# A delta-rule attention with two MLPs: the opening in one given order on all engines, the state in SBUF, PSUM as two pairs, three merged insertions a chunk

## The chip, the cores and the metric

The kernel runs on 1 core of a Trainium2 chip. The metric is the device time of one execution in microseconds (us). The engines are TensorE (PE, matmuls), VectorE (DVE), ScalarE (ACT), GpSimd (POOL) and SyncE (SP, which here only issues DMAs). Each engine works through its own instruction queue in order and waits on semaphores of the others.

## The reference

Four batches with eight heads go through a delta rule over 768 tokens, one 48 x 48 state per batch and head. Its output, laid out as 3072 tokens by 384, goes through two MLPs with a hidden width of 2048.

```python
k_n = k / (norm(k) + 1e-06)
for t in range(S):                      # S = 768
    y[:, :, t] = q_t @ state
    v_old = state^T k_t
    state = state + beta_t * outer(k_t, v_t - v_old)
x = y as (3072, 384)
h = x @ w_in ; g = 0 if h <= -1, h if h >= 1, else (h + 1) ** 2 / 4 ; x = g @ w_out
h = x @ w_in2; g = max(h, 0) ** 2                                   ; x = g @ w_out2
```

The weights arrive as 64-bit floats, so that each must be turned into 32-bit words on the chip first.

## The kernel before

**Attention.** The tokens are cut into 12 chunks of 64, and two chunks make a group. For each chunk there are these pieces of PE work: `keys_gram` (kk, the keys' Gram matrix), `scores` (kq), `ks` (state times keys, subtracted from the values in kv), `tr` (the solved triangular matrix times kv), `qs` (the queries' part of yy), `ku` (the update of the state), `pu` (the scores' part of yy), and two `xt` (transposes of the result into the MLP's input xh, xl). For each group there is a triangular solve, `tri`: transposes of the Gram matrix on DVE (`begin`, tile gm), nine small operations with a square root on ACT (`pre`), 30 elimination steps with two operations each (`steps`; on DVE for group 0, on POOL for the others), and transposes back (`turned`, tiles tt and tq). Then `join1` (z, copied to zs by ACT) and `join2` (x) join the two 32-token halves of a chunk. The state is summed up in two PSUM banks (`s_ps`) and copied to the SBUF tile st after each chunk.

**MLP.** 24 units of 128 tokens form 9 blocks of two or three units (`UNITS`) in layer 0 and 8 blocks of three in layer 1. A step x (called a unit of work in the code after) handles one of 16 slices f of the hidden width for one block: `hidden` makes h with 9 matmuls (each operand is split into a high and a low part, and three of the four products are taken), the activation runs over ACT and DVE (r, g), then g is split into gh (ACT) and gl (DVE), and two steps later (`LAG`) `out1` or `out2` adds 9 matmuls into three accumulators acc0 to acc2. After 16 steps `evac` copies the accumulators to a tile e and sends them out.

**Weights.** Each of the 32 layer-0 tiles (128 x 384) comes as a raw 64-bit tile by DMA. ACT prepares its two words (two instructions, L185 and L189), DVE joins them to a 32-bit word (L196, tile wl), ACT casts the high part (L207), DVE subtracts it to get the low part (L211). At most two raw loads are under way (`FLIGHT`), and the beta loads are issued by ACT's queue.

**What sets the order.** Attention is inserted between the steps of the MLP at slots, two slots a step: `put_a` (exa) for PE work and `put` (exb) for the rest. PE's order is that of the code everywhere. For the other engines a scheduler, which fills their queues by its own timeline, decides from chunk 0's join on; only the loads, the Gram products and the first solve stand in a given order. The weights' stages are fed in by `more_w1`.

**PSUM.** Eight banks: two for the state, acc0 to acc2, h, and one pair (att0, att1) for all attention products.

Of the kernel before, what the change touches and what calls it, by code (L numbers as in the profile page):

```python
# [23 lines left out]
UNITS = [2, 2, 3, 3, 3, 3, 3, 2, 3]  # L24
# [3 lines left out]
def kernel(  # L28
# [9 lines left out]
    nc = tc.nc  # L38
# [16 lines left out]
    EAGER = 18  # L55
    AHEAD = 8
    FLIGHT = 2
# [5 lines left out]
    HEAD = 6  # L63
# [36 lines left out]
    def pair(shape, name):  # L100
        tags = PAIRS[0]
        if start[0]:
            tags = PAIRS[turn[0] % 2]
            turn[0] += 1
        return [ps.tile(shape, F32, tag=t, name=name) for t in tags]

    def single(shape, name):
        tag = (SINGLES if start[0] else PAIRS[0])[turn[1] % 2]
        turn[1] += 1
        return ps.tile(shape, F32, tag=tag, name=name)  # L110
# [21 lines left out]
    def load_kg(c):  # L132
        if c >= NCH:
            return
        t = kqg[c] = ring.tile([P, 2, H, T], F32, tag="kqg", bufs=2, name="kqg")
# [17 lines left out]
    def load_bet():  # L153
        src = beta.rearrange("(b o r) g (s t) -> o s b r g t", b=B2, o=2, s=2)
        for o in range(2):
            for s in range(2):
                for b2 in range(B2):
                    p = 64 * o + L * s + GC * H * b2
                    nc.scalar.dma_start(bet[p:p + GC * H], src[o, s, b2, 0:GC * H])

    raws = {}
    sent = []

    def load_w(x, key):
# [5 lines left out]
        ins = nc.sync.dma_start(  # L170
            raw.rearrange("p a b -> p (a b)"), (w1, w2)[w][f, i].bitcast(I32)
        ).ins
        if w == 0:
            sent.append(ins)
            if len(sent) > FLIGHT:
                tc.add_manual_dep(
                    ins, sent[-1 - FLIGHT].name,
                    mybir.DependencyInfo(mybir.DependencyClass.Sync, mybir.DependencyReason.DATA),
                    reason="at most FLIGHT weight loads under way",
                )  # L180

    def convert_stages(key, box):
        def s0():
            raw = box["raw"] = raws.pop(key)
            nc.scalar.activation(  # L185
                raw[:, :, 1].bitcast(F32), raw[:, :, 1].bitcast(F32), AF.Prelu,
                scale=2.0 ** -112, alpha=2.0 ** 32,
            )
# [4 lines left out]
        def s1():  # L193
            raw = box.pop("raw")
            box["t"] = tmp("wl", WL)
            nc.vector.scalar_tensor_tensor(  # L196
                box["t"].bitcast(I32), raw[:, :, 1], 3, raw[:, :, 0],
                ALU.logical_shift_left, ALU.bitwise_or,
            )

        return [s0, s1]

    def part_stages(key, box):
        _, f, i = key

        def s3():
            nc.scalar.copy(weight(i, f)[0], box["t"])  # L207

        def s4():
            hi, lo = weight(i, f)  # L210
            nc.vector.tensor_sub(lo, box["t"], hi.bitcast(F32))  # L211

        return convert_stages(key, box) + [s3, s4]
# [3 lines left out]
    def weight_items(w):  # L217

        keys = [(w, f, i) for f in range(NF) for i in range(2)]
        if w == 0:  # L220
            keys.sort(key=lambda k: (k[1] + LAG * k[2], -k[2]))

        def item(x):
            _, f, i = keys[x]
            box = {}
            if w == 0:
                r = part_stages(keys[x], box)
            else:
                r = convert_stages(keys[x], box)
                r.append(lambda: nc.sync.dma_start(w2f[f, :, i], box["t"]))  # L230
            s1 = r[1]
            r[1] = lambda: (s1(), ahead(x + 1 + (RAW if w else AHEAD)))
# [4 lines left out]
        def ahead(end):  # L237
            while todo and todo[0][0] < end:
                load_w(*todo.pop(0))
# [57 lines left out]
    def keys_gram(c, late=False):  # L297
# [4 lines left out]
        o_ = pair([P, H, 2 * L], "kk")  # L302
# [39 lines left out]
    def scores(c, late=False):  # L342

        p_ = pt[c] = ring.tile([P, B2, H, T], F32, tag="pt", bufs=1, name="pt")
        o_ = pair([P, H, T], "kq")
# [5 lines left out]
        for b2 in range(B2):  # L351
            if late:
                nc.scalar.copy(p_[:, b2], o_[b2])
            else:
                nc.vector.tensor_mul(p_[:, b2], o_[b2], by)

        def keep():
            for b2 in range(B2):
                nc.gpsimd.tensor_mul(p_[:, b2], p_[:, b2], by)

        return keep

    def tri(n, eng):
# [9 lines left out]
        def begin():  # L373
            nc.vector.transpose(gm.rearrange("p j i -> p i j"), packed)
# [51 lines left out]
    def turned(n):  # L426
        tag, bufs = ("gm", 1) if n else ("kqt", 2)
        tq[n] = ring.tile([P, B2, GC, H, L], F32, tag=tag, bufs=bufs, name="tq")
        nc.vector.transpose(tt[n][..., 0:L].rearrange(lanes), tx)
        nc.vector.transpose(tq[n].rearrange(lanes), tx.rearrange("p j i -> p i j"))  # L430
# [14 lines left out]
    def join2(n, js):  # L445
        o_ = pair([P, len(js), H, L], "x")
# [16 lines left out]
    def chunk_steps(c):  # L463
# [3 lines left out]
        def ks():  # L467
            o_ = pair([P, H, D], "ks")
# [7 lines left out]
        def tr():  # L476
            o_ = pair([P, H, D], "tr")
# [6 lines left out]
        def qs():  # L484
            o_ = t["y"] = pair([P, H, D], "yy")
# [7 lines left out]
            load_kq(c + 2)  # L493

        def ku():
            if c == NCH - 1:
                return
            flat = kvt[c].rearrange("p x h d -> p (x h d)")
            w = 64 if c == 0 else D
            each(lambda h, b2, o: mm(  # L500
                s_ps[o][rows(b2, w), h],
                flat[rows(b2 ^ o), DM * o + D * h:DM * o + D * h + w],
                kvt[c][rows(b2 ^ o), 2 + o, h],
                c == 0 and h == 0, c == NCH - 2,
            ))
            nc.vector.tensor_copy(st[:, 0], s_ps[0])
            t["st"] = nc.scalar.copy(st[:, 1], s_ps[1]).ins

        def pu():
            if c == 0:  # L510
                t["y"] = pair([P, H, D], "yy")
            if c == NCH - 1:
                for b2 in range(B2):
                    nc.scalar.copy(kvt[c][:, b2], t["y"][b2])
                t["y"] = pair([P, H, D], "yy")
            o_ = t["y"]


            each(lambda h, b2, o: mm(
                o_[b2][rows(o), h], pt[c][rows(b2 ^ o), b2, h], kvt[c][rows(b2 ^ o), 2 + o, h],  # L520
                c in (0, NCH - 1) and h == 0, behind=t.get("st") if h + b2 + o == 0 else None,
# [3 lines left out]
        def yy():  # L525
            to = kvt[c][:, 0:2]
            if c == 0:
                to = wp.tile([P, 2, H, D], F32, tag=f"w1{NF - 1}", name="y")
            for b2 in range(B2):
                if c == NCH - 1:  # L530
                    nc.vector.tensor_add(to[:, b2], to[:, b2], t["y"][b2])
                else:
                    nc.scalar.copy(to[:, b2], t["y"][b2])
            t["to"] = to

        def qk():
            qs()
            ku()

        def py():  # L540
# [23 lines left out]
        if c == 0:  # L564
            return tr, py, lambda: (ku(), done()), xt
        return ks, tr, qk, py, xt
# [17 lines left out]
    def hidden(layer, n, f):  # L584
        w = xh[n].shape[2]
        many = start[0] or (layer, n) >= (0, NB - 1) or n == 0 and f < MANY
        bank = ("h", "att0", "att1")[f % 3] if many else "h"
# [9 lines left out]
        if layer == 0:  # L597
            marks[0] = nc.scalar.activation(r, h, AF.Relu, bias=one)  # L598
            marks[1] = nc.vector.tensor_scalar(g, r, 2.0, 0.5, ALU.min, ALU.mult)  # L599
# [333 lines left out]
```

## Time and profile before

| what | us |
| --- | --- |
| three runs | 1102.3, 1111.05, 1114.37 |
| median | 1111.05 |
| profiled execution, device time | 1104.04 |
| its span from first to last instruction | 1102.3 |
| busy: PE, DVE, ACT, POOL | 965.9, 623.1, 500.0, 272.3 |
| mean granted clock of PE | 0.981 of full speed |

The share of busy time is a mean over stages with different limits. So the rows below are taken by stage: the opening up to the first MLP matmul, block zero of the MLP, the rest of layer 0, and layer 1. A busy time counts the instruction's time on the engine, with what it waits for a port in it.

### The profile page before, as it was taken

Reading aid. Unit: us, or ns where it says so; the run is one execution under the profiler, and the core shown is the slowest. Engines: PE = TensorE matmul, PEld = TensorE weight load, DVE = VectorE, ACT = ScalarE, POOL = GpSimd, SP = SyncE. Lnnn points to the kernel's source line nnn. Section 1 sums busy time; section 2 is a strip of 40 time slices with the busy share of each in tenths; the row PEclk is TensorE's granted clock in tenths of the full one; section 3 lists DMA queues with packets and bytes.
Section 4 is the critical chain, followed back from the end, with each engine's and each line's share of the span. In section 5 each row is a group of like instructions: output and inputs, shape, how many; then the busy total and the mean of one; then the engine's idle time right before and its main releaser. Section 6 shows DMA issues by size and latency. Waiting matters only on the chain.

```text
span 1102.3 us, 28998 instructions
## 1 busy us (share of the span) xinstructions
PE 965.9 (88%) x12456; PEld 934.0 (85%) x12456; DVE 623.1 (57%) x1121; ACT 500.0 (45%) x1025; POOL 272.3 (25%) x385
## 2 busy tenths in 40 slices
PE   2103698989989899999899999999999999999998
PEld 2103588978988889889899999999999999999998
DVE  1868966757756664576554577744434343434333
ACT  1555545545546345554555555433333333333332
POOL 1318602833811760058000022310101010101000
PEclk9999899999999899999999999999999999999999
DMA  8871223542335134144201122301001010000000
GB/s 167 232 214 52 59 52 97 146 119 72 75 112 155 31 96 115 33 127 124 74 3 42 63 65 84 103 1 43 21 23 44 1 44 1 23 1 22 1 22 22
DMA packets 53128, 76.67 MB, mean 70 GB/s; under 512 B 20616, under 2 KB 40456, under 8 KB 53000
## 3 DMA queue, kind: packets, MB, share of 16 engines
q1 hardware_dynamic: 52104, 74.73, 24.5%
q8 instruction: 97, 1.59, 0.6%
q10 hardware_dynamic: 896, 0.10, 0.1%
q14 instruction: 31, 0.25, 0.1%
HBM read 59.08 MB, written 15.73 MB: 68 GB/s over the span
## 4 chain that ended last, share of the span: by engine, by line
PE 69%; DVE 12%; DMA 9%; ACT 4%; issue 3%; POOL 2%; SPq 1%; DVEq 0%; ACTq 0%
PE h L574 31%; PE acc L574 31%; DMA raw<-in_w_dram 5%; PE yy L289 2%; DVE g L601 2%; DVE g L599 2%; DMA x<-e 2%; DVE wl L196 1%; DVE w L211 1%; DMA bet<-in_beta_dram 1%; DVE gl L610 1%; PE kq L289 1%; POOL t L412 1%; DMA kv<-in_kv_dram 1%; POOL tx L416 1%
## 5 line engine op out<-in xcount | busy, mean ns | idle before, releaser
L574 PE MATMUL h<-xh,w 128*128 128x384 f32 (+1 forms) x1632 | 322.6, 334 | 4.5 <-ACT r L598 3.5
L574 PEld LDWEIGHTS h<-xh,w 128*128 128x128 f32 x1632 | 278.1, 193 | 7.9 <-ACT r L598 4.3
L610 DVE TENSOR_TENSOR gl<-g,gh 128x384 fp32r<-128x384 f32 (+1 forms) x272 | 167.0, 614 | 136.3 <-ACT gh L609 130.8
L609 ACT CAST gh<-g 128x384 fp32r<-128x384 f32 (+1 forms) x272 | 134.5, 494 | 191.0 <-DVE g L601 88.8
L574 PE MATMUL h<-xl,w 128*128 128x384 f32 (+1 forms) x816 | 180.4, 330 | 0.0
L574 PE MATMUL acc<-gh,w 128*128 128x384 f32 (+1 forms) x864 | 167.7, 329 | 12.3 <-DVE e L617 8.0
L604 DVE TENSOR_TENSOR g<-r 128x384 f32<-128x384 f32 x128 | 71.3, 557 | 157.7 <-ACT r L603 157.6
L574 PE MATMUL acc<-w,gh 128*128 128x384 f32 x768 | 155.6, 337 | 1.9 <-DVE e L617 1.9
L574 PEld LDWEIGHTS acc<-gh,w 128*128 128x128 f32 x864 | 138.8, 191 | 17.5 <-DVE e L617 8.6
L603 ACT ACTIVATE r<-h,zero 128x384 f32<-128x384 f32 x128 | 74.4, 581 | 166.5 <-PE h L574 166.5
L574 PEld LDWEIGHTS h<-xl,w 128*128 128x128 f32 x816 | 142.4, 191 | 0.0
L574 PEld LDWEIGHTS acc<-w,gh 128*128 128x128 f32 x768 | 136.3, 188 | 2.2 <-ACT gh L609 2.2
L598 ACT ACTIVATE r<-h,one 128x384 f32<-128x384 f32 (+1 forms) x144 | 78.5, 545 | 83.0 <-PE h L574 81.4
L601 DVE SCALAR_TENSOR_TENSOR g<-r,g 128x384 f32<-128x384 f32 (+1 forms) x144 | 85.1, 591 | 46.0 <-ACT g L600 44.3
L599 DVE TENSOR_SCALAR g<-r 128x384 f32<-128x384 f32 (+1 forms) x144 | 66.1, 459 | 75.9 <-ACT r L598 75.2
L600 ACT ACTIVATE g<-g 128x384 f32<-128x384 f32 (+1 forms) x144 | 70.3, 488 | 66.2 <-DVE g L599 65.6
L574 PE MATMUL acc<-gl,w 128*128 128x384 f32 (+1 forms) x432 | 92.6, 323 | 6.4 <-DVE gl L610 6.4
L412 POOL TENSOR_TENSOR t<-tx,gm 128x30 f32<-128x30 f32 (+9 forms) x150 | 91.8, 612 | 17.1 <-DVE tx L402 5.8
L660 POOL CAST xh<-x2r 128x1152 fp32r<-128x1152 f32 x8 | 9.4, 1173 | 346.7 <-PE h L574 346.6
L416 POOL TENSOR_TENSOR tx<-tx,t 128x30 f32<-128x30 f32 (+9 forms) x150 | 90.5, 603 | 11.7 <-DVE tx L403 0.2
L574 PE MATMUL acc<-w,gl 128*128 128x384 f32 x384 | 88.0, 337 | 0.0
L574 PEld LDWEIGHTS acc<-gl,w 128*128 128x128 f32 x432 | 73.2, 192 | 7.2 <-DVE gl L610 7.2
(101 smaller groups left out, 880.5 us busy)
## 6 DMA issues: line engine op xcount, KB each, us to landing
raw<-in_w_dram SPq DMA_DIRECT2D x64, 384.0 KB, 3.7
kqt<-in_kq_dram SPq DMA_DIRECT2D x24, 384.0 KB, 6.5
w2f<-wl SPq DMA_DIRECT2D x32, 192.0 KB, 3.7
w2r<-w2f SPq DMA_DIRECT2D x16, 384.0 KB, 3.5
kv<-in_kv_dram SPq DMA_DIRECT2D x12, 384.0 KB, 3.4
x2r<-x SPq DMA_DIRECT2D x8, 576.0 KB, 4.3
out_dram<-e SPq DMA_DIRECT2D x24, 192.0 KB, 2.0
kqg<-in_kq_dram SPq DMA_DIRECT2D x40, 96.0 KB, 3.8
```

The costliest lines, as they stand in the source:

```text
L289: ins = nc.tensor.matmul(o, l, r, start=start, stop=stop, skip_group_check=True).ins
L412: eng.tensor_mul(t, x[:, 0:j, j:j + 1].to_broadcast([P, j, w]), gm[:, j:j + 1, j + 1:L].to_broadcast([P, j, w]),)
L416: eng.tensor_add(rest, rest, t)
L574: nc.tensor.matmul(o, *((r, l) if swap else (l, r)), **flags)
L598: marks[0] = nc.scalar.activation(r, h, AF.Relu, bias=one)
L599: marks[1] = nc.vector.tensor_scalar(g, r, 2.0, 0.5, ALU.min, ALU.mult)
L600: nc.scalar.activation(g, g, AF.Square)
L601: nc.vector.scalar_tensor_tensor(g, r, -1.0, g, ALU.add, ALU.max)
L603: marks[0] = nc.scalar.activation(r, h, AF.Relu, bias=zero)
L604: marks[1] = nc.vector.tensor_mul(g, r, r)
L609: nc.scalar.copy(ghi, g)
L610: nc.vector.tensor_sub(glo, g, ghi.bitcast(F32))
```

## The change

1. **The opening in one given order.** All engines follow the order of the code up to the end of block zero (16 steps). ACT issues no DMA any more; the beta loads go group by group through SP. The raw loads stand one after the other in SP's queue, without the limit of two. ACT prepares 18 raw tiles between the solve and zs, and the first three weight tiles are cast and subtracted by POOL. In block zero the function `between` puts two more tiles into each step: tile a is cast by ACT, tile b by POOL, and DVE joins and subtracts both.
2. **The state in SBUF.** `ku` writes its product to a PSUM pair, and DVE adds it to st (four instructions of 48 partitions; copies for chunk 0).
3. **PSUM as two pairs**, A (a0, a1) and Z (b0, b1). `ks` uses A and `scores` Z; `qs` uses Z and `tr` A; `ku` uses A and `pu` adds to Z. The other tiles rotate over all four. In layer 1 h rotates over five banks instead of three.
4. **Three merged insertions a chunk** in place of five: `one` (ks and scores), `two` (qs and tr), `three` (ku, pu and the copies).
5. The Gram tiles are evacuated by ACT and masked by POOL (`late=True`) throughout. The transposes of a solve are cut into quarters, and those back are spread over four slots, from the fifth slot ahead of the join on. The evacuation e has two buffers of its own (`ev`) for two of three accumulators. `UNITS` has its third two-unit block at place three instead of place eight.

```diff
-UNITS = [2, 2, 3, 3, 3, 3, 3, 2, 3]
+UNITS = [2, 2, 2, 3, 3, 3, 3, 3, 3]
...
-    s_ps = [ps.tile([P, H, D], F32, name=f"sps{i}") for i in range(2)]
...
-    PAIRS = [("att0", "att1"), ("acc0", "acc1")]
-    SINGLES = ["acc2", "h"]
...
+    A, Z = ("a0", "a1"), ("b0", "b1")
...
     def turned(n):
...
+        q = [slice(x * L // 4, (x + 1) * L // 4) for x in range(4)]
+        return [
+            lambda t=t, o=o, i=i: nc.vector.transpose(t[:, i], o[:, i])
+            for t, o in zip(to, of) for i in q
+        ]
...
+        def one():
+            o_ = pair([P, H, D], "ks", A)
...
+            keep = scores(c, Z)
             for b2 in range(B2):
                 r = kvt[c][:, 2 + b2]
                 nc.vector.tensor_sub(r, r, o_[b2])
+            keep()
...
+        def two():
+            o_ = t["y"] = pair([P, H, D], "yy", Z)
...
+            tr()
...
+            k_ = pair([P, H, D], "ku", tags)
             each(lambda h, b2, o: mm(
...
+                k_[o][rows(b2, D), h], flat[rows(b2 ^ o), o, D * h:D * (h + 1)],
+                kvt[c][rows(b2 ^ o), 2 + o, h], h == 0,
             ))
-            nc.vector.tensor_copy(st[:, 0], s_ps[0])
-            t["st"] = nc.scalar.copy(st[:, 1], s_ps[1]).ins
...
+                            nc.vector.tensor_add(st[r, o], st[r, o], k_[o][r])
...
+        def three():
             ku()
...
     def evac(i, o, dst):
-        e = ring.tile(list(o.shape), F32, tag="wl", bufs=WL, name="e")
+        tag, bufs = ("wl", WL) if i == 2 else ("ev", 2)
+        e = ring.tile(list(o.shape), F32, tag=tag, bufs=bufs, name="e")
...
+    def between(f):
+        a, b = (tiles + [None] * NW)[2 * f:2 * f + 2]
...
+            if x == 0:
+                if last_low:
+                    lower(last_low.pop(), V)
+                if a is not None:
+                    make(a)
+                some(2)
+            elif x == 1:
+                if a is not None:
+                    upper(a, nc.scalar.copy)
+                if b is not None:
+                    make(b)
+                    upper(b, G.tensor_copy)
+                    last_low.append(b)
+            elif x == 2:
+                some(1)
+            elif a is not None:
+                lower(a, V)
...
         go(steps)
-        turned(0)
+        for x in range(EARLY - 2):
+            whole_bits(x)
+        value(0)
         go(masks)
...
+            put(0, z - 5, *later(*[lambda fs=fs: go(fs) for fs in in_pairs(lambda: turned(g))]))
...
+        for x in range(NF):
+            unit(x, between(x))
+    with tc.manual_schedule(engines={mybir.EngineType.PE}):
+        for x in range(NF, total):
+            unit(x)
```

`make` is DVE's join, `upper` the cast, `lower` the subtraction, `halves` and `whole_bits` ACT's two preparing instructions, `some(m)` the next m of those for the last twelve tiles.

ACT's queue at its start, before and then after. In the names st is the solve's small tile behind the square root, tt and pt are copies out of PSUM, bet is beta.

```order
L159 DMA bet<-in_beta_dram 16x6x32 x8
L712 ACT_TABLE_LOAD
L712 ACTIVATE st<-one,zero 128x1
L332 COPY tt<-kk 128x8x32 x2
L185 ACTIVATE raw<-raw 128x384
L189 ACTIVATE raw<-raw 128x384
L332 COPY tt<-kk 128x8x32 x2
L185 ACTIVATE raw<-raw 128x384
L189 ACTIVATE raw<-raw 128x384
L267 ACTIVATE st_319<-gm,tiny 128x32
```

```order
L789 ACT_TABLE_LOAD
L789 ACTIVATE st<-one,zero 128x1
L329 COPY tt<-kk 128x8x32 x4
L264 ACTIVATE st_345<-gm,tiny 128x32
L326 COPY tt<-kk 128x8x32
L329 COPY tt<-kk 128x8x32
```

The beta loads and two raw tiles stood ahead of the square root; now nothing but the copies of the first two chunks does. All 18 raw tiles come behind it, and right behind them zs (L449).

DVE's queue in block zero, before from the evacuation of the first step's h, and then after. L599 and L606 are the first operation on r, L601 and L609 the second, L610 and L620 make gl; L196 and L188 are the joins, L211 and L217 the subtractions.

```order
L599 TENSOR_SCALAR g<-r 128x256
L196 SCALAR_TENSOR_TENSOR wl<-raw 128x384
L211 TENSOR_TENSOR w_1094<-wl,w_1094 128x384
L211 TENSOR_TENSOR w_1103<-wl,w_1103 128x384
L601 SCALAR_TENSOR_TENSOR g<-r,g 128x256
L196 SCALAR_TENSOR_TENSOR wl<-raw 128x384
L211 TENSOR_TENSOR w_1142<-wl,w_1142 128x384
L196 SCALAR_TENSOR_TENSOR wl<-raw 128x384
L599 TENSOR_SCALAR g<-r 128x256
L610 TENSOR_TENSOR gl<-g,gh 128x256
```

```order
L403 TENSOR_TENSOR tx<-gm,st_689 128x512
L404 COPY tx<-st_689 128x32
L606 TENSOR_SCALAR g<-r 128x256
L188 SCALAR_TENSOR_TENSOR wl<-raw 128x384
L609 SCALAR_TENSOR_TENSOR g<-r,g 128x256
L188 SCALAR_TENSOR_TENSOR wl<-raw 128x384
L620 TENSOR_TENSOR gl<-g,gh 128x256
L217 TENSOR_TENSOR w_949<-wl,w_949 128x384
L519 COPY st<-ku 48x384 x2
L606 TENSOR_SCALAR g<-r 128x256
```

The weights' work was as dense before, but about half of it stood ahead of the first step and nearly all the rest in the next seven; now two tiles go with each step up to the fifteenth, and the second solve's preparation (up to L404) stands ahead of the first step.

PE's queue around the first two insertions of chunk 2, before and then after; h, acc and w are the MLP's tiles.

```order
L289 MATMUL ks<-st,kqt 64x48 x32
L574 MATMUL h<-xh,w_905 128x256 x6
L574 MATMUL h<-xl,w_905 128x256 x3
...
L289 MATMUL kq<-kqt 64x64 x32
L574 MATMUL h<-xh,w_919 128x256 x6
```

```order
L286 MATMUL ks<-st,kqt 64x48 x32
L286 MATMUL kq<-kqt 64x64 x32
L580 MATMUL h<-xh,w_1535 128x256 x6
L580 MATMUL h<-xl,w_1535 128x256 x3
...
L286 MATMUL yy<-st,kqt 64x48 x32
L286 MATMUL tr<-kv,tt 64x48 x32
```

kq moved up to ks, into the other pair of banks; in the same way qs now stands right ahead of tr.

## Rows read from the trace of the kernel before

**Rows 1.** Busy by stretch: length, each engine's busy us (instructions), clock, DMA share, GB/s
```profile
0.00:66.00 66.00, 13.37 (x640) 11.06 (x640) 37.93 (x79) 23.69 (x54) 14.37 (x33) 1.00 0.82 201
...
88.00:140.00 52.00, 26.93 (x454) 23.57 (x458) 49.32 (x80) 27.48 (x62) 37.15 (x50) 0.93 0.15 39
106.00:172.00 66.00, 53.56 (x1110) 49.20 (x1111) 53.33 (x102) 34.91 (x83) 20.79 (x29) 0.92 0.26 58
172.00:700.00 528.00, 493.86 (x8233) 470.13 (x8231) 337.56 (x618) 274.39 (x573) 183.21 (x272) 0.97 0.31 86
700.00:1102.00 402.00, 397.49 (x2277) 397.19 (x2277) 167.66 (x282) 143.64 (x267) 30.19 (x17) 1.00 0.07 23
```
**Rows 2.** Timeline, first solve: start, us, engine, line, tiles [idle before <-releaser]
```profile
17.57 2.12 DVE L374 STREAM_TRANSPOSE gm<-tt 128x1024 f32<-128x1024 f32 x1
...
26.26 0.54 ACT L185 ACTIVATE raw<-raw 128x384 f32<-128x384 f32 x1 [9.06 <-DMA raw<-in_w_dram]
...
28.54 0.35 ACT L267 ACTIVATE st<-gm,tiny 128x32 f32<-128x32 f32 x1
...
34.23 0.18 DVE L412 TENSOR_TENSOR t<-tx,gm 128x30 f32<-128x30 f32 x1
...
63.05 1.96 DVE L430 STREAM_TRANSPOSE tq<-tx 128x1024 f32<-128x1024 f32 x1
```
**Rows 3.** Timeline of ACT around zs, and the chain's last raw tile
```profile
76.86 0.54 ACT L185 ACTIVATE raw<-raw 128x384 f32<-128x384 f32 x1 [0.69 <-DMA raw<-in_w_dram]
...
77.73 0.37 ACT L443 ACTIVATE zs<-z 128x256 f32<-128x256 f32 x1
...
84.12 3.80 DMA raw<-in_w_dram
```
**Rows 4.** Timeline of PE and ACT from zs to the first MLP matmul
```profile
84.84 2.29 PE L289 MATMUL tr<-kv,tt 64*64 64x48 f32 x64 [5.61 <-POOL tx L416]
...
93.94 1.95 PE L289 MATMUL yy<-kv,pt 64*64 64x48 f32 x62 [0.74 <-DVE kv L482]
...
102.79 0.85 ACT L533 COPY y<-yy 128x384 f32<-128x384 f32 x2
...
103.31 1.54 PE L552 MATMUL xt<-ident,y 128*128 128x128 f32 x6 [7.42 <-ACT y L533]
105.86 1.41 PE L574 MATMUL h<-xh,w 128*128 128x256 f32 x5 [1.00 <-DVE xl L555]
```
**Rows 5.** DVE's groups, 88 to 140 us: count, busy us, mean ns, idle before
```profile
L196 DVE SCALAR_TENSOR_TENSOR wl<-raw 128x384 int32<-128x384 int32 x26 | 21.2, 826 | 0.0
```
**Rows 6.** DVE's groups from 140 to 172 us, when POOL is idle
```profile
L610 DVE TENSOR_TENSOR gl<-g,gh 128x256 fp32r<-128x256 f32 x10 | 4.2, 423 | 3.2 <-ACT gh L609 2.7 <-PE kq L289 0.5
...
L599 DVE TENSOR_SCALAR g<-r 128x256 f32<-128x256 f32 x9 | 2.6, 294 | 6.1 <-ACT r L598 6.1
...
L211 DVE TENSOR_TENSOR w<-wl,w 128x384 fp32r<-128x384 f32 x2 | 1.0, 552 | 0.0
```
**Rows 7.** PE's waits, 172 to 700 us: us in total, times, longest
```profile
PE acc L574 <- DVE e L617: 8.0, 4, 2.9
PE z L289 <- DVE tt L429: 6.9, 4, 3.2
PE z L289 <- DVE tq L430: 5.9, 4, 1.5
PE kq L289 <- DVE kv L474: 5.6, 4, 2.8
```
**Rows 8.** Timeline of PE, the first matmuls of block one
```profile
171.81 0.84 PE L574 MATMUL h<-xh,w 128*128 128x256 f32 x6
```
**Rows 9.** PE's groups, 172 to 700 us, the Gram products of six chunks
```profile
L289 PE MATMUL kk<-kqg 48*32 48x64 f32 x768 | 9.4, 225 | 1.5 <-issue 1.5
```
**Rows 10.** Timeline, third solve: its transposes on DVE and POOL's last step
```profile
179.44 2.18 DVE L374 STREAM_TRANSPOSE gm<-tt 128x1024 f32<-128x1024 f32 x1 [0.29 <-ACT tt L456]
...
228.57 0.28 POOL L416 TENSOR_TENSOR tx<-tx,t 128x30 f32<-128x30 f32 x1
```

More of the change, by code (lines that the diff above doesn't have):

```diff
@@ L169, in load_w @@
         raw = raws[key] = pool.tile([P, DM, 2], I32, tag=tag, bufs=bufs, name="raw")
[L170 to L180, printed above, removed]
+        nc.sync.dma_start(raw.rearrange("p a b -> p (a b)"), (w1, w2)[w][f, i].bitcast(I32))
     def convert_stages(key, box):
@@ L191, in s0, with joined_words, halves, whole_bits @@
             )
[L193 to L213, printed above, removed]
-    w2f = dram.tile([NF, P, 2, DM], F32, name="w2f", bufs=1)
[L217 to L221, printed above, removed]
+        return high, low
+    def joined_words(t, raw):
+        nc.vector.scalar_tensor_tensor(
+            t.bitcast(I32), raw[:, :, 1], 3, raw[:, :, 0],
+            ALU.logical_shift_left, ALU.bitwise_or,
+        )
+    w2f = dram.tile([NF, P, 2, DM], F32, name="w2f", bufs=1)
+    order = [(0, f, i) for f in range(NF) for i in range(2)]
+    order.sort(key=lambda k: (k[1] + LAG * k[2], -k[2]))
+    words = {}
+    def halves(x):
+        return sign_bits(raws[order[x]])
+    def whole_bits(x):
+        for f in halves(x):
+            f()
+    def make(x):
+        words[x] = tmp("wl", WL)
+        joined_words(words[x], raws.pop(order[x]))
+    def upper(x, copy):
+        _, f, i = order[x]
+        copy(weight(i, f)[0], words[x])
+    def lower(x, eng):
+        _, f, i = order[x]
+        hi, lo = weight(i, f)
+        eng.tensor_sub(lo, words.pop(x), hi.bitcast(F32))
+    def weight_items():
+        keys = [(1, f, i) for f in range(NF) for i in range(2)]
         def item(x):
@@ L683 @@
     V, G = nc.vector, nc.gpsimd
-    first1, w1s = weight_items(0)
-    first2, w2s = weight_items(1)
-    w1f = flow(w1s)
-    w1f.reverse()
+    first2, w2s = weight_items()
+    whole = list(range(GC))
+    SL = 2 * NF
     SPREAD = 3
-    behind = [nullcontext]
-    def more_w1(m=1):
-        with behind[0]():
-            for _ in range(m):
-                if w1f:
-                    w1f.pop()()
-    whole = list(range(GC))
+    NW = len(order)
+    EARLY, READY = 20, 3
+    exa, exb = {}, {}
@@ new lines, with some, part @@
+    todo1 = [f for x in range(EARLY, NW) for f in (lambda x=x: halves(x)[0](), lambda x=x: halves(x)[1]())]
+    todo1.reverse()
+    tiles = list(range(READY, NW))
+    last_low = []
+    def some(m):
+        for _ in range(m):
+            if todo1:
+                todo1.pop()()
+    def between(f):
+        a, b = (tiles + [None] * NW)[2 * f:2 * f + 2]
+        def part(x):
+            if x == 0:
[15 more added lines that the diff above has]
+                lower(a, V)
+        return part
@@ new lines, in put, with later, one_, in_pairs @@
+    def put(n, slot, *fs):
+        for i, f in enumerate(fs):
+            exb.setdefault(SL * n + slot + i, []).append(f)
+    def later(*fs):
+        def one_(f):
+            with tc.issue_after(marks[0].ins), tc.issue_after(marks[1].ins):
+                f()
+        return [lambda f=f: one_(f) for f in fs]
+    def in_pairs(fs):
+        box = []
+        def piece(i):
+            if not box:
+                box.extend(fs())
+            go(box[2 * i:2 * i + 2])
+        return [[lambda i=i: piece(i)] for i in range(4)]
@@ new lines, in put_a, with run, out_, unit @@
+    def put_a(n, slot, f):
+        exa.setdefault(SL * n + slot, []).append(f)
+    def run(ex, x):
+        for f in ex.pop(x, ()):
+            f()
+    blocks = [(0, n) for n in range(NB)] + [(1, n) for n in range(NM)]
+    total = NF * len(blocks)
+    def out_(x):
+        g, f = divmod(x, NF)
+        (out1, out2)[blocks[g][0]](blocks[g][1], f)
+    def unit(x, between=lambda x: None):
+        g, f = divmod(x, NF)
+        rest = hidden(*blocks[g], f, between)
+        run(exa, 2 * x)
+        rest()
+        run(exb, 2 * x)
+        if x >= LAG:
+            out_(x - LAG)
+        run(exa, 2 * x + 1)
+        run(exb, 2 * x + 1)
```

355 lines of the change are left out of this document (166 added, 189 removed).

## The prediction

> **What bounds the kernel now.** I read the busy time by stretch first [rows 1]. From 172 us on TensorE (PE) is the bound: 493.9 of 528 us in the rest of layer 0, 397.5 of 402 us in layer 1. Before that it is not: from 106 to 172 us it works 53.6 of 66 us, and the first MLP matmul comes only at 105.86 us [rows 4]. Block one of the MLP begins at 171.8 us [rows 8]. So a change can gain in two places: how early PE fills up, and the 34 us in which PE idles between 172 and 700 us (with the 3% of that stretch at the lower clock level).
>
> The timeline tells what the opening waits for. The first triangular solve runs on VectorE (DVE): its transposes start at 17.57 us, but the square root that it needs next runs only at 28.54 us, after a raw weight tile's conversion that had waited for its DMA [rows 2]. The solve's steps run from 34.23 us and the last transpose ends at 63.05 + 1.96 = 65.0 us [rows 2]. The z product needs nothing that is later, but ScalarE (ACT) copies it to zs only at 77.73 us, since conversions of raw tiles, each waiting for its DMA, stand ahead of it [rows 3]; the last raw tile lands at 84.12 + 3.80 = 87.9 us [rows 3]. From zs to the first MLP matmul at 105.86 us pass 28.1 us, though the links are short: tr 2.29, yy 1.95, two copies 0.85, xt 1.54 us [rows 4]. Between them DVE and ACT make weight tiles. From 88 to 140 us DVE is busy 49.3 of 52 us [rows 1].
>
> **Part 1: the solve and zs.** ACT no longer issues the beta loads, and the fixed order puts the square root ahead of all raw tiles. I leave the transposes at 17.57 us, end them at 19.7 us, and the root moves from 28.54 to 19.7 us: 8.8 us. The rest of the solve keeps its 36.5 us (28.54 to 65.0), so it ends at 56.2 us, and z a microsecond later (64 short matmuls, at half of tr's 64). Now ACT must have finished 18 raw tiles before zs. The 32 raw tiles took from 26.26 to 87.9 us, 1.93 us each with two under way [rows 2, 3]; the eighteenth then lands at about 26.3 + 17 x 1.93 = 59.1 us, and its pair of conversions takes 1.0 us [rows 3]. With eight under way it can come faster; what the DMA engines could give beyond their 82% before 66 us [rows 1] bounds it at 53 us. I take zs at 58.5 us: 19.2 us earlier. Bounds: 57 and 61 us.
>
> **Part 2: zs to the first MLP matmul.** In the fixed order only three weight tiles stand in this stretch, mostly on GpSimd (POOL). Chain: zs 0.4, x products and copies 2.0, tr 2.3, copy 0.6, yy 2.0, copies 0.9, ku 2 (priced as yy), xt 1.5 [rows 4]; with the waits between engines 12 us. First h at 70.5 us instead of 105.86. But the second solve's preparation now stands on DVE ahead of the first MLP evacuation. Its cost is that of the first one, 34.23 - 28.54 = 5.7 us [rows 2]; its root can run on ACT while DVE still subtracts for xl, for which I take off 0.7 us: DVE enters block zero at 75.5 us.
>
> **Part 3: block zero.** This is where the saving is paid for. Before, weight tiles were made in DVE's gaps from 78 us on; now 29 of 32 are made inside block zero, two a unit. DVE's work there: 58 joins and subtractions at 0.55 us = 32 us, sixteen units with three 256-wide operations at 0.29, 0.42 and 0.42 = 18 us (both two-input ones at the one row shown), and some 15 attention operations, 8 us: 58 us [rows 6]. That is without POOL. While POOL ran its solve before (50 operations in 52 us [rows 1]), the same join took 0.83 us [rows 5]; DVE's 80 operations of that stretch (53 joins and subtractions, 19 of a unit's, 8 others), at the durations of [rows 6], come to 40.4 us and took 52: a factor of 1.29. In block zero POOL has some 66 operations (48 of the solve, 14 casts, the values and masks), so I keep the factor: 58 x 1.29 = 75 us. Block one starts at 75.5 + 75 = 150.5 instead of 171.8 us: 21.3 us gained. Bounds: 58 us if nothing collides, and 58 + 66 x 0.74 = 107 us if every POOL operation (0.74 us in [rows 1]) runs alone.
>
> The Trainium skill, "SBUF — State Buffer", section "Who interferes with whom", says that DVE and GpSimd share a port pair under an exclusive lock, and the loser blocks for a whole instruction. By it the casts moved to POOL would cost DVE what they save, and block one would start at about 182 us. The trace agrees only in part: by this rule the 88 to 140 us stretch would need 40.4 + 37.2 = 77.6 us and it took 52. I take the row.
>
> **Part 4: from block one on.** PE's matmuls stay, but one Gram product more lies behind block zero: 9.4 / 6 = 1.6 us [rows 9]. The waits of PE there [rows 7]: 12.8 us for the two transposes ahead of z, which now come in quarters five slots earlier; 8.0 us for the evacuation of the accumulators, whose buffers no longer share a ring with the weights (two of three); 5.6 us for kq behind kv, since scores now has its own PSUM pair and no evacuation between. I leave 4, 2 and 1 us of them. The second join stays tight: the solve took 49 us before, from 179.44 to 228.85 us [rows 10], behind 17 units of the MLP by the order of instructions, and has 14 now. So 19.4 us come back; some 3 us of clock more, as fewer gaps let the clock fall (0.97 over 528 us is 8 us lost) [rows 1]. Against this stands the state in SBUF: four additions a chunk on DVE instead of one copy, 2 us each chunk; DVE is busy 338 of 528 us, so they hide, but they and the doubled waits of a merged insertion may delay the next one: 2.5 us over ten chunks. Net 20 us. If DVE's slack were gone, the additions would cost 10 x 1.6 = 16 us. Evacuating the Gram tiles moves from DVE to ACT and POOL (274 and 183 of 528 us busy): nothing. Five PSUM banks for h in layer 1 bring nothing, since PE idles 4.5 of 402 us there, most of it the tail.
>
> **Sum**, against the profiled execution: 1102.3 - 21.3 + 1.6 - 20 = 1062.6 us. That execution lies 0.8% under the median of the three runs shown (1111.05); I forecast 1063.
>
> **The rivals.**
> - *Block zero without collisions.* POOL's casts wait for DVE's joins, so the two may alternate instead of collide. 58 us instead of 75: 1046 us. For it: DVE's waits for ACT are the only other hold. Against it: [rows 5]. 15%.
> - *Exclusive lock.* 107 us: block one at 182.5 us, later than before, total 1095. Against it the 52 us above. 15%.
> - *The steady waits are replaced, not removed*: the turning blocks DVE's queue while it waits for POOL, and a merged insertion waits for two evacuations. Opening as forecast, nothing behind: 1102.3 - 21.3 + 1.6 = 1083 us. 13%.
> - *The order is no help.* Raw tiles gate zs as before, or the fixed order waits where the scheduler would have gone past: block one at 172 to 185 us, some of part 4 back: 1100 to 1115 us. 7%.
> - *Slower: lockstep in block zero.* Three engines in one given order hand each unit round: ACT 3.4 us (relu, square, two casts, three half conversions), DVE 3.0 us and 1.7 us of collisions, nothing overlapped: 8.1 us a unit. Then block one starts at 75.5 + 15 x 8.1 + 10 = 207 us, and the total is 1102.3 + 35 + 1.6 - 20 = 1119 us. It decides from a unit of 7.2 us up (block one at 193 us, where part 4 is eaten up). For it: every cast, square and join of a unit waits for another engine. Against it: LAG = 2 lets PE run on, and the joins need nothing of the unit. 8%.
>
> **How the numbers follow.** The forecast has 42% and by itself 1050 to 1076 us (a unit 0.8 us cheaper or dearer in block zero). About 1% is what a measurement of this kernel can tell from no change, so under 1100 us is faster: 42 + 15 + 13, and half of the lock's 15, is 78%. Within 1%: the rest of the lock and the useless order, 14%. Slower 8%. The range leaves out the lockstep, the useless order and the fast end of the first rival: 1038 to 1097 us.
>
> **What would show it.** zs between 57 and 61 us; the first h near 70; block one's first h near 150, with DVE over 90% busy between 75 and 145 us; PE's waits for DVE's transposes and for e under 6 us together; layer 1 unchanged at 402 us. A first h beyond 80 us means that raw tiles gate; a block zero with DVE under 75% busy means lockstep; PE waits for yy, tr or ku mean that the merged insertions took the waits over.

## The result and the profile after

| kernel | median us (runs) | kernel before beside it | ratio, 95% interval |
| --- | --- | --- | --- |
| after | 1063.31 (4) | 1109.82 | 0.9582 [0.9521, 0.9643] |
| after, a second time | 1063.70 (6) | 1109.03 | 0.9587 [0.9557, 0.9616] |

The change makes the kernel 4.2% faster; 1063 us was forecast. The profiled execution of the kernel after has a span of 1063.0 us, that of before 1102.3 us. The medians lie 46.5 us apart, 7 us more: the profiled execution of before is a quick one (1104.04 us, median 1109.82). Where these 7 us lie no profile shows; where the 39.3 us lie is read from three stretches: up to the first matmul of block one, from there to layer 1's first activation, and layer 1. The busy times by stretch of the kernel after (columns as in [rows 1]):

```profile
74.25:147.89 73.64, 54.88 (x907) 50.52 (x907) 67.79 (x119) 40.86 (x98) 45.60 (x61) 0.80 0.22 50
147.89:655.90 508.01, 485.40 (x8342) 464.84 (x8343) 349.87 (x670) 270.27 (x574) 197.39 (x302) 0.98 0.32 89
655.90:1063.00 407.10, 400.98 (x2298) 400.36 (x2297) 172.61 (x289) 146.31 (x273) 32.26 (x19) 0.99 0.08 25
```

And the last two stretches of the kernel before, cut at the same places:

```profile
171.81:695.01 523.20, 490.43 (x8216) 467.02 (x8215) 332.77 (x611) 271.86 (x567) 181.17 (x270) 0.97 0.31 86
695.01:1102.30 407.29, 401.11 (x2298) 400.50 (x2297) 172.48 (x289) 146.28 (x273) 32.23 (x19) 1.00 0.08 25
```

Block one starts 171.81 - 147.89 = 23.9 us earlier; the stretch behind it is 523.2 - 508.0 = 15.2 us shorter; layer 1 is the same (407.3 and 407.1 us). In the middle stretch PE has 126 matmuls more (the Gram product that moved behind block zero), and both parts of its time fell: idle from 32.8 to 22.6 us, busy from 490.4 to 485.4 us, which with more matmuls is the clock (0.97 to 0.98).

The opening in the timeline of the kernel after (start, length, engine, line, tiles, idle time before and its releaser; the rows come from several engines), to be held against [rows 2 to 4, 8]:

```profile
19.43 0.35 ACT L264 ACTIVATE st<-gm,tiny 128x32 f32<-128x32 f32 x1 [2.01 <-DVE gm L373]
...
44.44 0.53 ACT L181 ACTIVATE raw<-raw 128x384 int32<-128x384 uint32 x1
...
52.57 2.13 DVE L434 STREAM_TRANSPOSE tq<-tx 128x256 f32<-128x256 f32 x4
...
55.89 0.38 ACT L449 ACTIVATE zs<-z 128x256 f32<-128x256 f32 x1 [10.93 <-PE z L286]
...
69.67 0.92 PE L580 MATMUL h<-xh,w 128*128 128x256 f32 x6 [0.66 <-ACT xh L560]
...
74.16 0.20 DVE L404 COPY tx<-st 128x32 f32<-128x32 f32 x1 [0.51 <-POOL tx L403]
...
77.05 1.11 DVE L519 COPY st<-ku 48x384 f32<-48x384 f32 x2
...
78.31 1.62 PE L580 MATMUL h<-xh,w 128*128 128x256 f32 x6 [7.36 <-DVE st L519]
...
147.89 0.97 PE L580 MATMUL h<-xh,w 128*128 128x256 f32 x6 [0.89 <-ACT r L605]
```

The square root comes 9.1 us earlier, and ACT is through with its 18 raw tiles at 45.0 us and idles 10.9 us before zs: there zs waits for the solve, no longer for raw tiles. DVE enters block zero at 74.25 us, and the second h waits 7.4 us for a copy of the state (L519), which was not in the forecast.

PE's waits of the kernel after in the middle stretch, 147.89 to 655.90 us (us in total, times, longest):

```profile
PE h L580 <- ACT r L605: 7.1, 10, 1.4
PE yy L286 <- DVE pt L354: 6.6, 7, 2.4
PE z L286 <- issue: 2.1, 1, 2.1
PE acc L580 <- DVE e L629: 0.4, 1, 0.4
```

And one more of the kernel before, beside those of [rows 7], which have the same totals between 171.81 and 695.01 us:

```profile
PE h L574 <- ACT r L598: 2.4, 1, 2.4
```

The waits of z for DVE's transposes (12.8 us) and of kq (5.6 us) are gone, that of acc fell from 8.0 to 0.4 us. Two others grew: yy waits 6.6 us for the masks of the scores, whose bank pair it needs, and h waits 7.1 us for r instead of 2.4. "issue" marks gaps for which the profile shows no releaser: 7.1 us here, 2.3 us before.

### The profile page after: what moved, and what is told of

Its sections match the earlier page's. It is cut to its first block, busy times and chain, and to the rows that moved or that the text cites. A ratio compares the mean times of both kernels' runs of the same rounds, so it can differ in the third digit from the quotient of the medians.

```text
span 1063.0 us, 29107 instructions
## 1 busy us (share of the span) xinstructions
PE 963.9 (91%) x12456; PEld 935.1 (88%) x12456; DVE 636.3 (60%) x1186; ACT 489.0 (46%) x1014; POOL 294.4 (28%) x421
## 4 chain that ended last, share of the span: by engine, by line
PE 75%; DVE 14%; ACT 5%; issue 3%; DMA 1%; SPq 1%; POOL 0%; DVEq 0%; ACTq 0%; POOLq 0%
PE h L580 33%; PE acc L580 32%; DVE g L609 2%; PE yy L286 2%; DVE g L606 2%; DVE gl L620 2%; PE tr L286 1%; PE kk L286 1%; DVE tx L417 1%; ACT gh L618 1%; DVE t L413 1%; ACT g L608 1%; DVE w L217 1%; PE ks L286 1%; PE kq L286 1%
## 5 line engine op out<-in xcount | busy, mean ns | idle before, releaser
L620 DVE TENSOR_TENSOR gl<-g,gh 128x384 fp32r<-128x384 f32 (+1 forms) x272 | 167.8, 617 | 133.1 <-ACT gh L618 129.7
L580 PEld LDWEIGHTS acc<-gh,w 128*128 128x128 f32 x864 | 142.2, 196 | 5.2 <-issue 1.7
L609 DVE SCALAR_TENSOR_TENSOR g<-r,g 128x384 f32<-128x384 f32 (+1 forms) x144 | 87.8, 610 | 37.9 <-ACT g L608 36.5
L606 DVE TENSOR_SCALAR g<-r 128x384 f32<-128x384 f32 (+1 forms) x144 | 69.9, 486 | 48.1 <-ACT r L605 47.3
L413 POOL TENSOR_TENSOR t<-tx,gm 128x30 f32<-128x30 f32 (+9 forms) x150 | 88.0, 587 | 11.5 <-DVE tx L403 1.3
```

The lines of the kernel that those rows point to most:

```text
L413: eng.tensor_mul(t, x[:, 0:j, j:j + 1].to_broadcast([P, j, w]), gm[:, j:j + 1, j + 1:L].to_broadcast([P, j, w]),)
L580: nc.tensor.matmul(o, *((r, l) if swap else (l, r)), **flags)
L609: nc.vector.scalar_tensor_tensor(g, r, -1.0, g, ALU.add, ALU.max)
L620: nc.vector.tensor_sub(glo, g, ghi.bitcast(F32))
```

## The experiments

**Does GpSimd stretch DVE in block zero? (e1)** The second group's solve keeps only its first elimination step; the other 29 are left out.

```diff
-        for i, f in enumerate(steps):
+        for i, f in enumerate(steps[:1]):
             put(0, 3 + 5 * i // 4, f)
```

> Leaves out 29 of the 30 elimination steps of the second group's solve, so GpSimd does 58 operations less in block zero (the output of two chunks is not the reference's). Collision theory (DVE's work is stretched there by what GpSimd does beside it): block zero falls from 74.4 us to 60-64 us, DVE's join falls from 778 ns to under 650 ns, total 1049-1053 us. Rival A (DVE's own number of operations or a round trip between ACT and DVE sets the unit): block zero stays at 72-75 us, total 1061-1064 us. Rival B (every GpSimd operation blocks DVE for its whole length): 58 x 0.72 us = 42 us off, block zero under 45 us or at PE's own 57 us, total near 1046 us.

Measured: 1056.64 us, ratio 0.9543 [0.9491, 0.9595], between the theory's range and rival A's; the profiled execution is the quickest of the four, with a span of 1051.5 us. Its block one starts at 137.93 us, 10.0 us earlier (9.1 us against the second execution of the kernel after). Its row from 74.25 us to there:

```profile
74.25:137.93 63.68, 50.29 (x907) 46.77 (x907) 56.12 (x119) 40.24 (x98) 17.32 (x22) 0.95 0.24 52
```

DVE's groups from 88 to 140 us (count, busy us, mean ns), first of the kernel after, then of e1:

```profile
L188 DVE SCALAR_TENSOR_TENSOR wl<-raw 128x384 int32<-128x384 int32 x23 | 17.9, 778 | 0.0
L217 DVE TENSOR_TENSOR w<-wl,w 128x384 fp32r<-128x384 f32 x22 | 16.2, 738 | 0.0
L609 DVE SCALAR_TENSOR_TENSOR g<-r,g 128x256 f32<-128x256 f32 x11 | 6.7, 611 | 0.0
L606 DVE TENSOR_SCALAR g<-r 128x256 f32<-128x256 f32 x11 | 5.7, 518 | 0.8 <-ACT r L605 0.7
L620 DVE TENSOR_TENSOR gl<-g,gh 128x256 fp32r<-128x256 f32 x11 | 5.3, 479 | 0.5
L521 DVE TENSOR_TENSOR st<-st,ku 48x384 f32<-48x384 f32 x4 | 2.0, 547 | 0.0
L354 DVE TENSOR_TENSOR pt<-kq,after 128x512 f32<-128x512 f32 x2 | 1.3, 682 | 0.0
```

```profile
L217 DVE TENSOR_TENSOR w<-wl,w 128x384 fp32r<-128x384 f32 x25 | 16.7, 669 | 0.0
L188 DVE SCALAR_TENSOR_TENSOR wl<-raw 128x384 int32<-128x384 int32 x25 | 15.0, 599 | 0.0
L620 DVE TENSOR_TENSOR gl<-g,gh 128x256 fp32r<-128x256 f32 x13 | 6.0, 465 | 1.0 <-ACT gh L618 0.3
L609 DVE SCALAR_TENSOR_TENSOR g<-r,g 128x256 f32<-128x256 f32 x14 | 5.9, 419 | 0.5 <-ACT g L608 0.5
L606 DVE TENSOR_SCALAR g<-r 128x256 f32<-128x256 f32 x14 | 4.5, 325 | 1.8 <-ACT r L605 1.7
L521 DVE TENSOR_TENSOR st<-st,ku 48x384 f32<-48x384 f32 x4 | 2.0, 546 | 0.0
L354 DVE TENSOR_TENSOR pt<-kq,after 128x512 f32<-128x512 f32 x2 | 1.3, 680 | 0.0
```

The join falls from 778 to 599 ns, the unit's L609 from 611 to 419 and L606 from 518 to 325 ns, while the two that read an operand from PSUM (L521, L354) stay as they were. So the collisions are real, and those that they hit have all their inputs in SBUF. Not each that has is hit: L620 (two such inputs) falls only from 479 to 465 ns, and why isn't shown. The price of the collisions: from DVE's entry (74.25 us) to block one GpSimd is busy 45.6 us in the kernel after, and 17.3 us between the same two moments in e1. The 28.3 us taken away gave back 10.0 us, a third. They are 39 instructions (x61 and x22), not the 58 of the expectation: the other steps that e1 leaves out lie behind block zero. That makes 0.26 us each. The exclusive lock would have given back all 28.3 us, or at least brought block zero down to PE's own 55 us; it stands at 137.93 - 74.25 = 63.7 us. Rival A (no effect) and rival B (the lock) both fall.

The Trainium skill, "SBUF — State Buffer", section "Who interferes with whom", says that a DVE instruction with two SBUF inputs contends with GpSimd's reads, and one with at most one SBUF input, outside the two-port modes, does not. On which operations are hit, the trace agrees for L188 and L609 against L521 and L354, and hardly for L620. L606 has one SBUF input and is hit; whether it runs in a two-port mode no run here shows. That the loser blocks for a whole instruction does not add up to GpSimd's whole busy time here: 10.0 us of 28.3.

**Did the limit of two loads hold zs back? (e2)**

```diff
+        if w == 0:
+            sent.append(ins)
+            if len(sent) > 2:
+                tc.add_manual_dep(ins, sent[-3].name, ...)
```

> At most two raw weight loads under way again, as in the kernel before; all else as after. If that limit had held the loads at 1.93 us a tile: the eighteenth conversion ends near 61 us, zs goes from 55.9 to 60-62 us, first h from 69.7 to 74-76 us, total +4 to +6 us. If the loads then starve block zero as well (32 tiles at 1.93 us end at 88 us, they are needed two a unit of 4.65 us from 74 us on): no more than that. Rival (only the order of ACT's queue mattered, the loads came as fast as the DMA engines can): zs and total unchanged within 1 us.

Measured: 1062.47 us, ratio 0.9571 [0.9539, 0.9602], the same as after. ACT's first and last raw tile and zs in e2:

```profile
28.05 0.56 ACT L189 ACTIVATE raw<-raw 128x384 f32<-128x384 f32 x1
...
55.47 0.54 ACT L192 ACTIVATE raw<-raw 128x384 int32<-128x384 uint32 x1
55.91 0.36 ACT L460 ACTIVATE zs<-z 128x256 f32<-128x256 f32 x1
```

The limit does slow the loads: from 30 to 50 us they run at 212 GB/s with a DMA share (the time that packets took, as a share of 16 engines' time) of 0.75, against 373 GB/s and 1.04 without it. But the eighteenth tile is done at 56.0 us, just when z is there. So the order of ACT's queue is enough to move zs: before, 25 raw tiles stood ahead of zs on ACT, now 18. Dropping the limit brought nothing measurable.

**Casts back on ACT (e3)**

```diff
-                upper(b, G.tensor_copy)
+                upper(b, nc.scalar.copy)
```

> Tile b of each step of block zero is cast by ACT too, 14 casts less on GpSimd. Collision theory: 58 us of DVE work are stretched to 75 us by some 66 GpSimd operations, 0.26 us each, so 14 less give back 3 to 4 us: block zero 70-71 us, total 1059-1060 us. Rival (the hand-over ACT to DVE is as tight as DVE's work): 14 x 0.51 us = 7 us more on ACT, block zero 74-81 us, total 1063-1070 us.

Measured: 1068.05 us, ratio 0.9626 [0.9593, 0.9659], 4 to 5 us slower; block one starts at 155.88 us, 8.0 us later. DVE in e3 from 74 to 156 us:

```profile
L188 DVE SCALAR_TENSOR_TENSOR wl<-raw 128x384 int32<-128x384 int32 x29 | 20.3, 702 | 0.0
L620 DVE TENSOR_TENSOR gl<-g,gh 128x256 fp32r<-128x256 f32 x15 | 7.0, 464 | 11.4 <-ACT gh L618 11.4
```

DVE's operations did get shorter, as the collision theory wants (the join 702 ns, 744 in the same stretch of the kernel after), but DVE now idles 11.4 us behind ACT's gh (0.3 us in the kernel after). The rival holds: block zero stands between two limits, DVE's work and the round trip through ACT, and 7 us more on ACT tip it over. The lockstep that I had priced as a slower case is near; the casts on GpSimd keep the kernel out of it.

**The second h's wait (e4)**

```diff
         xt0(0)
         xt0(1)
+        states()
...
-        put(0, 1, states)
```

> The copies of the first state (four, 48 partitions) stand behind the first chunk's last transposes, ahead of the second solve's preparation, instead of behind the first step of block zero. Theory: the second h waits 7.4 us for the bank that these copies free; the wait goes, DVE's work stays the same, but DVE's first operation on r comes 1.1 us later. If that wait holds block zero back: block zero's last step 3 to 6 us earlier, total 1057-1060 us. Rival (DVE is the bound in block zero, and it does the same work, so PE's wait at its start costs nothing): the wait goes and is found elsewhere in block zero, total 1062-1064 us.

Measured: 1059.40 us, ratio 0.9538 [0.9504, 0.9572]. The wait of 7.4 us is gone and block one starts at 143.33 us, 4.6 us earlier (3.7 us against the second execution of the kernel after), which the span (1058.1 us) shows in full. The rival falls: though DVE does the same work, it had itself idled 3.0 us behind that second h. Of the single edits with the whole output it alone is faster than the kernel after by more than 1 us: ratio 0.954 against 0.958 and 0.959. The intervals of these ratios overlap; the gain is read from the stage.

**Transposes back whole, one slot ahead of the join (e5)**

```diff
-            put(0, z - 5, *later(*[lambda fs=fs: go(fs) for fs in in_pairs(lambda: turned(g))]))
+            put(0, z - 1, *later(lambda: go(turned(g))))
```

> The transposes back of every solve are whole again and stand one slot ahead of the join, as in the kernel before; all else as after. Theory (the quarters, four slots earlier, removed z's waits): z's waits for them come back, 2.5 to 3.2 us for each of five groups, 10 to 15 us of PE idle time behind block zero and total +8 to +14 us, 1071 to 1077 us. Rival (what removed the waits was that the two-unit block or DVE's lighter queue lets the solve end earlier): total +0 to +3 us, z's waits under 4 us.

Measured: 1072.44 us, ratio 0.9668 [0.9601, 0.9735], 9 us slower. PE's waits in e5 between 147 and 672 us, and its middle stretch:

```profile
PE yy L286 <- DVE pt L354: 9.2, 11, 2.7
PE z L286 <- DVE tq L433: 5.7, 5, 1.5
PE z L286 <- DVE tt L433: 2.9, 2, 1.9
```

```profile
147.89:671.69 523.80, 491.42 (x8342) 471.87 (x8343) 348.49 (x640) 272.16 (x574) 198.89 (x306) 0.96 0.32 87
```

z's waits come back with 8.6 us, yy's grow by 2.6 us: idle 32.4 us instead of 22.6. Busy time grows by 6.0 us at the same number of matmuls (0.96 against 0.98 of full clock). The profiled execution was the slowest of its four, so by the medians the two together are 9, not 15.8 us. The quarters and their earlier slots together are worth that (the edit takes back both); the rival falls.

**Evacuations in the weights' ring (e6)**

```diff
-        tag, bufs = ("wl", WL) if i == 2 else ("ev", 2)
+        tag, bufs = "wl", WL
```

> All three evacuations e share the weights' ring of three buffers again, as in the kernel before; all else as after. Theory: PE's wait of acc for e grows from 2.3 to about 8 us, total +4 to +6 us, 1067 to 1069 us. Rival (the ring is no hold, since layer 0's later weights use it rarely): acc's wait under 4 us, total within 2 us of 1063.

Measured: 1071.46 us, ratio 0.9661 [0.9607, 0.9715], 8 us slower, more than expected, and only in part by the wait that was named (PE's waits and its row, both in the middle stretch):

```profile
PE h L580 <- ACT r L605: 9.1, 9, 2.8
PE yy L286 <- DVE pt L354: 6.4, 6, 2.4
PE acc L580 <- DVE e L629: 3.7, 5, 1.5
```

```profile
147.09:663.89 516.80, 489.94 (x8342) 468.39 (x8343) 350.99 (x670) 270.68 (x575) 197.93 (x303) 0.97 0.32 87
```

acc's wait for e grows from 0.4 to 3.7 us, most of the idle time that comes back: PE idles 26.9 us instead of 22.6. (The 2.3 us of the expectation hold 1.9 us that lie in layer 1; the kernel before has the same 1.9 us there, outside its 8.0.) So the ring does hold acc, for 3.3 us where about 6 were expected. The other half of the loss is busy time, 489.9 us instead of 485.4 at the same number of matmuls (0.97 against 0.98 of full clock); the executions of e9 and e12 below differ as much (488.1 and 482.8 us) without a cause that is known, so it isn't shown to come from the ring. The rival had the size of the wait (under 4 us) and not the total.

**Masks on GpSimd against yy's wait (e7)**

```diff
-            keep = scores(c, Z)
+            keep = scores(c, Z, late=True)
```

> The score products are copied out of PSUM by ACT and masked by GpSimd in SBUF (four operations a chunk in place of two on DVE), so that bank pair Z comes free before DVE has done the subtractions and masks. Theory: PE's wait of yy for the masks (6.6 us in seven times) goes, total -3 to -6 us, 1057 to 1060 us. Rival: yy then waits for ACT's copies, which stand behind the steps' own casts, 3 to 6 us again; or the last score product waits for GpSimd, whose masks stand behind the solve's steps; total 1062 to 1068 us.

Measured: 1096.23 us, ratio 0.9882 [0.9828, 0.9936]: 33 us slower than the kernel after, some 70% of the change's gain of 46.5 us.

```profile
PE yy L286 <- POOL pt L352: 36.8, 6, 14.7
PE h L580 <- ACT r L605: 5.8, 8, 1.4
```

The wait of yy for DVE's masks is gone, but the product of the scores (the second part of yy) now waits for GpSimd, whose masks stand behind the solve's steps, up to 14.7 us. The rival named the place; its size was far off (1062 to 1068 us). GpSimd is idle more than half of this stretch, and its queue is still the wrong place for anything that PE needs soon.

**Four weight tiles ahead of the first step (e8)**

```diff
-    EARLY, READY = 20, 3
+    EARLY, READY = 20, 4
...
+        make(3)
+        upper(3, G.tensor_copy)
+        lower(2, V)
```

> First state's copies early as in the run that moved them (1059.4 us), and four weight tiles ready ahead of the first step instead of three: DVE, which idles some 9 us between 58 and 69 us, joins four and subtracts three, GpSimd subtracts the fourth. One tile less in block zero: 1.1 us of DVE work stretched by 1.29. Theory (DVE's work sets block zero): 1.4 us less than with the early copies alone, 1057 to 1058.5 us. Rival (the extra DVE work delays the chain from zs to the first step): first h 1 to 3 us later than 68.7 us, total 1059 to 1062 us.

Measured: 1058.32 us, ratio 0.9536 [0.9474, 0.9599]. The first h comes at 70.74 us (68.66 in e4), as the rival said, and block one at 145.49 us (143.33): it starts as much later as the first h does, so that one tile less saved nothing between the two. The total lies in the theory's range all the same, since the rest of the execution is shorter than in e4; a difference from e4 can't be told.

**Masks ahead of the subtractions (e9), both (e10), and the kernel after again (e12)**

```diff
+            keep()
             for b2 in range(B2):
                 r = kvt[c][:, 2 + b2]
                 nc.vector.tensor_sub(r, r, o_[b2])
-            keep()
```

> In the merged insertion of ks and scores DVE masks the scores before it subtracts ks from the values (two lines exchanged), all else as after. Theory: yy's wait for bank pair Z (6.6 us in seven times between 152 and 662 us) is shortened by the two subtractions, 1.1 us each time, and tr's need for them is covered by yy's 1.1 to 2 us: PE's wait of yy 1 to 2 us, total 1057 to 1061 us. Rival: tr now waits for the subtractions as yy did for the masks, or the gain lies within what the clock gives and takes: total 1062 to 1064 us.

> The early state copies, the four weight tiles ahead of the first step, and the masks ahead of the subtractions together. If they add up: 5 us from the first two, 3 to 5 us from the third, total 1053 to 1056 us. If the third brings nothing: 1057 to 1059 us.

> The changed kernel once more, unaltered, on the same chip and beside the same runs of the kernel before as the three others: 1061 to 1065 us, ratio 0.953 to 0.963. What differs from its first profile shows how far one execution's clock and stages can be trusted: block zero 74 to 80 us, a clock there between 0.8 and 0.93.

Measured: e9 1066.34 us, 0.9620 [0.9592, 0.9648]; e10 1058.62 us, 0.9538 [0.9508, 0.9569]; the kernel after again 1063.70 us, 0.9587 [0.9557, 0.9616]. e9 did not test its theory. Behind block zero only PE follows the code's order; DVE's queue is the scheduler's, and it put the subtractions ahead of the masks as before. The two queues differ at one place, in block zero, and yy's wait stayed at 5.7 us. What e9 does show is the spread. Its middle stretch, and that of the kernel after in its second execution:

```profile
148.19:661.69 513.50, 488.09 (x8342) 468.31 (x8343) 350.88 (x670) 270.44 (x575) 199.25 (x306) 0.97 0.32 89
```

```profile
147.06:654.91 507.85, 482.76 (x8342) 462.93 (x8343) 351.71 (x670) 270.04 (x575) 200.06 (x306) 0.98 0.33 90
```

Two kernels with the same queues from block one on differ by 2.6 us in the median, and by 5.6 us in the middle stretch of one execution each, at the same idle time of PE (25.4 and 25.1 us). e10 is e8 again.

**UNITS as before (e11)**

```diff
-UNITS = [2, 2, 2, 3, 3, 3, 3, 3, 3]
+UNITS = [2, 2, 3, 3, 3, 3, 3, 2, 3]
```

> The list of units per block of the kernel before (the third two-unit block at place eight instead of place three), all else as after. A block of two units carries 16 steps over less PE work than one of three. Place three means that the third chunk pair's solve has fewer columns to hide behind, but also that one attention chunk's insertions are spread over shorter steps. Theory: only where the shorter steps lie changes, the solves were in time in both: total 1061 to 1066 us. Rival: with three units in block two the second join waits less, PE idles less behind block one: 1057 to 1061 us; or the last blocks of layer 0, which run at full clock without attention, suffer from a two-unit block: 1066 to 1072 us.

Measured: 1067.67 us, ratio 0.9632 [0.9597, 0.9667]. Its middle stretch is 6.7 us longer than that of the kernel after, all of it idle time of PE (30.3 us instead of 22.6, busy 484.4 instead of 485.4). The gaps ahead of h without a releaser in the profile are 8.2 us (0.9 us in the kernel after):

```profile
PE h L580 <- issue: 8.2, 3, 3.6
```

With the spread that e9 shows, 4 us are at the edge of what can be told, and the cause stays open.

## Why the prediction was right, step by step

- **Part 1, zs at 58.5 us: 55.9 us.** The square root went to 19.4 us as forecast (19.7), and the solve took 35.3 us to its last transpose (36.5). The step that was wrong is the gate: 18 raw tiles were to end at 59 us; they ended at 45.0 us. Without a limit a tile costs ACT's own 0.94 us, at 373 GB/s; with the limit of two (e2) they would have ended at 56.0 us. The bound of 53 us, taken from the DMA share of 82%, was no bound.
- **Part 2, first h at 70.5, DVE in block zero at 75.5 us: 69.67 and 74.25 us.** The chain took 13.8 us instead of 12.
- **Part 3, block zero 75 us: 73.6 us.** DVE is busy 67.8 of 73.6 us, 92%, as the test asked. The mechanism and its size held: the forecast's 17 us over 66 GpSimd operations are 0.26 us each, e1 measured 10.0 us for 39, which is 0.26 as well (0.23 with the 9.1 us), and block zero has 61 of them. The factor of 1.29 behind it is rougher than that looks, since its 52 us held 2.7 us in which DVE idled [rows 1]. Two other terms were off and cancelled, which is luck. The 58 us of work are a sum of mean durations, but DVE's records overlap: in block zero the durations sum to 75 us in a busy time of 67.8. And DVE idles 5.8 us there, 3.0 us of it behind the second h, whose wait for the first state's copies (worth 4.6 us by e4) I had not seen.
- **Part 4, 18.4 us with the Gram product: 15.2 us.** The removed waits went further than forecast: z 12.8 to nothing that is put down to the transposes (4 forecast), e 8.0 to 0.4 (2), kq 5.6 to 0.2 (1). The mis-sized terms are the other two. I allowed 2.5 us for what the merged insertions would cost; yy for the masks took 6.6 us, h for r 4.7 us more, and gaps without a releaser 4.8 us more. So PE's idle time fell by 10.2 us (7.7 in the second execution), not by 17. The clock gave back more than the 3 us: busy time fell by 5.0 us (7.7) with some 1.6 us of matmuls more. The 8 us that I put as its whole loss were too few: 0.97 over 528 us is some 15 us of full clock. No run undoes the state in SBUF, the two pairs or the merged insertions by itself, so what each of them gives isn't shown; e5 and e6 bear out the terms of z and e.
- **Layer 1:** unchanged, as forecast.
- **The rivals.** No collisions (1046 us) and the exclusive lock (1095 us) both fall by e1. "Waits replaced, not removed" is true for more than half: some 26 us of waits for z, e and kq went, and some 16 us of others came (yy, h, gaps without a releaser). Lockstep did not occur, but e3 shows that 7 us on ACT bring its beginning.

So 2.6 us more than forecast came from the opening and 3.2 us less from the steady part, and the two errors cancelled in the total: that it was met within 1 us is luck. The sum was also taken off the quick profiled execution of before; measured by the medians the gain is 46.5 us, not 40.

## What to carry to other kernels

A given order pays where one engine's queue holds work that nobody waits for yet: here a square root and one small copy, taken out from behind raw tiles, moved zs by 21.8 us, while faster loads moved nothing. When products share PSUM pairs, ask for each pair who reads it last: the two new waits (7.4 us once, 6.6 us in seven times) are both for a late reader, and putting one such reader earlier in its queue gave about 4 us (e4). Before you move an operation on the path to another engine, look at what stands in that queue, not at how busy it is (e7).

## What the runs showed of the hardware that I had not expected

- The granted clock in the profile's rows can differ from what the matmuls show. From 74 to 90 us the kernel after has 0.62 in its first execution (0.50, the level of 1.2 GHz, up to 86 us, then 2.4 GHz) and 1.00 in its second:

```profile
74.00:90.00 16.00, 10.40 (x173) 9.70 (x173) 12.28 (x24) 9.35 (x22) 6.78 (x9) 0.62 0.04 10
```

```profile
74.00:90.00 16.00, 9.89 (x173) 9.18 (x173) 12.23 (x23) 9.86 (x23) 7.07 (x9) 1.00 0.03 9
```

But the second h took its 1.62 us in both, as long as at the lower level. The second execution, to be held against 69.67 and 78.31 us in the first:

```profile
69.17 1.62 PE L580 MATMUL h<-xh,w 128*128 128x256 f32 x6 [0.66 <-ACT xh L560]
77.80 1.62 PE L580 MATMUL h<-xh,w 128*128 128x256 f32 x6 [6.37 <-DVE st L519]
```

Where the two did differ is the first h, 0.92 and 1.62 us, both behind the same 26 us of idle PE during the solve and the same products after it. So where a row's clock matters, the time of a known group of matmuls tells more.
- Where PE is the bound, waits and clock can move together. From before to after idle time fell by 10.2 us and busy time by 5.0 us at more matmuls; in e5 idle time rose by 9.8 us and busy time by 6.0 us. But e9 lost some 5 us of clock at the same idle time, and in e11 idle time rose by 7.7 us and busy time fell by 1.0 us. So this is no rule.
- In the middle stretch PE shows gaps for which the profile gives no releaser, 2.3 us in the kernel before and 7 to 13 us in the kernels after, up to 3.6 us each, at other places in each kernel.
